# Block-sparse attention and a GELU layer on one core: the last output row in two column pieces, the x of eight pairs transposed by DMA, idle staging tiles reused

## The chip, the cores and the metric

One core of a Trainium2 chip. The metric is the device time of one execution in microseconds, the median of the runs; lower is better. Engines are named as in the profile: PE (TensorE; PEld is its weight load), DVE (VectorE), ACT (ScalarE), POOL (GpSimd) and SP (SyncE, which issues nearly all transfers).

## The reference, cut to what matters

Inputs q, k and v are 4 batches × 8 heads × 768 tokens × 64, in 32 bits. Each query looks at its own block of 64 keys and at the three best of the earlier blocks (by the dot product with the block's mean key), causally. The result is put into rows of 512 (8 heads × 64) and goes through a two-layer network with a hidden width of 2048.

```python
k_rep = k.reshape(B, H, n_blocks, block, D).mean(axis=3)
gate_scores = np.einsum('bhsd,bhnd->bhsn', q, k_rep)
...
top_idx = np.argsort(gate_scores, axis=-1)[..., -top_k:]
...
scores = scale * np.matmul(q, k.transpose(0, 1, 3, 2))
mask = mask & (pos[:, None] >= pos[None, :])
scores = np.where(mask, scores, -1000000000.0)
...
return np.matmul(attn, v).astype(np.float32)
...
h = x @ w_in
c = np.float32(np.sqrt(2.0 / np.pi))
g = 0.5 * h * (1.0 + np.tanh(c * (h + 0.044715 * h * h * h)))
return (g @ w_out).astype(np.float32)
```

## The kernel before, in words

The work is cut into **steps**, and the order in which they are issued is written out by hand in the string `ORDER` (lines 26 to 129). `do` (L979) runs the entries one by one. `u.6.2.0@0` is the step `u.6.2.0` with PSUM slot 0, `xc.8.0:v` the step `xc.8.0` on engine v (a = ACT, v = DVE, p = POOL). Since each engine takes its instructions in order, `ORDER` also sets the order on every engine and on SP's queue of transfers. Tiles come from pools with a fixed number of buffers; a step that needs a buffer waits until its last reader is done.

**Attention.** Two heads make a pair; batch b has the pairs 4b to 4b+3, 16 in all. The first four are worked on in groups of two (names with `0`, L187 to L703). For pairs 4 to 15 the steps are, in the names of `ORDER`:
- `d.p.x` (`load`, L397): q, k and v (x = 0, 1, 2) of the pair, two transfers each, into an `io` tile (pool of 9).
- `hn`, `ln` (L706, L713): q and k as a high and a low 16-bit half, scaled; on POOL, DVE or ACT.
- `zqh`, `zkh`, `zql` (`dma_t`, L723): transposes of these halves by DMA, one instruction on SP's queue for 128 × 768 elements (L728).
- `c0`, `c1` (L733): copies of the transposed q and k into `qk`; `v` (L747): v in 16 bits.
- `s`, `b`, `g`, `m`, `mt`, `mc` (L738 to L817): block sums of k, gate scores, choice of three blocks, transposed mask, mask rows copied into `qk`. `kp`, `gt`, `mt` and `xt` all live in one PSUM bank (pool `small`, one buffer).
- `k`, `x`, `a` (L823 to L862): scores on PE, exponentials on ACT, causal part on POOL. Scores, `pv` and `hps` share three PSUM slots of two banks (`@0` to `@2`).
- `p` (L864): attn times v. `n` (`normalise`, L646): DVE divides and writes `xn` (16 bits, two buffers).
- `xt` (`x_t`, L663): six PE transposes of 128 × 128 into the `small` bank. `xc` (`x_c`, L877): ACT or DVE copies them into `xT`, which holds x transposed, 128 × 4 × 3072.

**The network.** Tokens go in 12 chunks of 256, three to a batch; so chunks 3 to 5 read the pairs 4 to 7, chunks 6 to 8 the pairs 8 to 11, chunks 9 to 11 the pairs 12 to 15.
- `u.ch.dj.half` (`up`, L913): 8 matmuls of 256 columns from `w_in` and `xT` into `hps`; the fourth of each group of four reads the fourth pair of the batch.
- `y.ch.dj` (`gelu`, L930): ACT.
- `f.ch.ti.dj` (`down`, L938): 4 matmuls of 512 columns into `ops`, for row block ti (128 tokens). `ops` comes from the pool `opsp`, one bank.
- `o.ch.ti` (`out_c`, L950): ACT or DVE copies the bank into `osb` (pool of 2). `w.ch.ti` (`out_d`, L955): 256 KB to memory from SP's queue.

The weights come in 32 bits through tiles of the pool `w32` (7 buffers), early in the run. `dmN` (`idle`, L970) is filler for PE in the first 27 us: N matmuls of 128 columns on zeros, 144 in all. The end of `ORDER`:

```
f.11.0.1 f.11.0.2 y.11.3 f.11.0.3 o.11.0:a w.11.0 f.11.1.0 w.10.0 f.11.1.1 f.11.1.2 f.11.1.3
o.11.1:a w.11.1
```

Of the kernel before, what the change touches and what calls it, by code (L numbers as in the profile page):

```python
# [8 lines left out]
FP32 = mybir.dt.float32  # L9
# [32 lines left out]
g.0.2 b.1.2 u.0.2.1 y.0.0 u.0.1.0@1 m.0.2 u.0.1.1 k.1.1.0.0@0 y.0.2 v.0.1.1:p d.4.1 lw.out.3
v.1.1.0:a c.par.0 y.0.1 k.1.1.1.0@2 mt.0.2 cw.in.7:p a.0.1.1 a.1.1.1 hn0.4.0:p ma.1.1.0 p.0.1.0@1
p.0.1.2 cw.out.1:p mc.0.2:v ln0.4.0:v p.0.1.3 p.0.1.1 g.1.2 d0.0.4.2 x.1.1.1.0 x.1.1.0.0 f.0.0.0
n.0.1 k.0.2.1.0@1 k.0.2.0.0@2 ma.0.2.0 d.5.0 a.1.1.0 d0.1.4.2 x.0.2.0.0 v.1.1.1:p p.1.1.0@0 m.1.2
p.1.1.2 p.1.1.1 p.1.1.3 xt.0.1 k.0.2.0.1@2 n.1.1 x.0.2.1.0 hn1.4.0:p cw.out.2:p cw.in.6:p
cw.out.3:v xc.0.1:a k.0.2.1.1@1 ma.0.2.1 zql.4.0 mt.1.2 x.0.2.0.1 v.0.2.0:v mc.1.2:v k.0.2.1.2@0
f.0.0.1 xt.1.1 zqh.4.0 u.0.3.0@2 xc.1.1:v x.0.2.1.1 d.5.1 hn0.5.0:p ln1.4.0:v lw.out.6 d0.0.5.2
ln0.5.0:v k.0.2.0.2@1 ma.0.2.2 u.0.3.1 x.0.2.0.2 lw.out.5 x.0.2.1.2 s.4.0 b.4.0 u.1.0.0@1
u.1.1.0@0 c.ke.0.0:p g.4.0 y.0.3 lw.out.7 u.1.0.1 u.1.1.1 zql.5.0 cw.out.4:v m.4.0 zqh.5.0 zkh.4.0  # L50
u.1.2.0@2 u.1.2.1 hn1.5.0:p a.0.2.1 y.1.0 a.0.2.0 k.1.2.0.0@1 ln1.5.0:v d0.1.5.2 y.1.1 v.0.2.1:a
c.ke.0.1:p cw.out.5:v k.1.2.1.0@0 cw.out.6:p ma.1.2.0 y.1.2 x.1.2.1.0 c.par.1 s.5.0 b.5.0
x.1.2.0.0 p.0.2.0@2 p.0.2.1 p.0.2.2 p.0.2.3 f.0.0.2 mt.4.0 k.1.2.1.1@0 n.0.2 k.1.2.0.1@2 ma.1.2.1
# [79 lines left out]
def kernel(  # L133
# [9 lines left out]
    nc = tc.nc  # L143
    B, H, S, D = q.shape
# [880 lines left out]
```

## Time and profile before

| | us |
|---|---|
| median of 3 runs | 281.26 |
| lowest and highest run | 280.41 and 281.69 |
| profiled execution, first to last instruction | 278.3 |
| PE busy in it | 264.5 (95%) |
| ACT, DVE, POOL busy | 192.8, 139.3, 131.4 |
| `ops` matmuls (L944) and `hps` matmuls (L923) | 95.0 and 92.9 |
| DMA transposes (L728) | 36 |
| transfers of the main queue, share of 16 DMA engines | 65.6% |

The profile shows another execution than the three timed ones, and its span leaves out what lies before the first and after the last instruction; the median is 3.0 us above it. Busy times are unions: a matmul's row gives its whole duration, and since matmuls are pipelined, what one costs is the distance between the starts of two. In the chain of waits such distances are what is shown.

### The profile page before, as it was taken

To read this page: it belongs to the slowest core of one execution; us is meant where nothing else is said; L and a number is where in the kernel's file an instruction comes from. 1 tells how busy PE (TensorE), PEld (TensorE's weight loads), DVE (VectorE), ACT (ScalarE), POOL (GpSimd) and SP (SyncE) were. 2 spreads that over 40 slices of the span, in tenths; PEclk is the share of its full clock that TensorE was granted. 3 is DMA by queue.
4 is the path that set the end of the run, shared out by engine and by line. 5 is a ranking of instruction groups with operands and counts; after the bars stand their busy time and mean duration, and the time that the engine had idled before them with its cause. 6 is when DMAs were issued, how large, how long until landed. Compare 5 with 4: busy or idle time off the path is not lost.

```text
span 278.3 us, 7163 instructions
## 1 busy us (share of the span) xinstructions
PE 264.5 (95%) x2910; PEld 188.8 (68%) x2910; DVE 139.3 (50%) x431; ACT 192.8 (69%) x221; POOL 131.4 (47%) x193
## 2 busy tenths in 40 slices
PE   5899697999999999999999999999999999999994
PEld 5677583865787666886766756786676777756651
DVE  2697458786878686867376466553442010000000
ACT  1568487788699979958898876897887753412330
POOL 6447699899725488870825929400352200000000
PEclk9999799999999999999999999999999999999999
DMA  8998999999699887998998984803112101010102
GB/s 177 272 258 266 346 287 225 245 263 183 110 207 220 181 172 145 204 237 110 169 228 194 245 132 101 166 2 59 39 38 77 40 0 40 38 40 0 75 0 113
DMA packets 107872, 41.09 MB, mean 148 GB/s; under 512 B 96576, under 2 KB 100672, under 8 KB 107840
## 3 DMA queue, kind: packets, MB, share of 16 engines
q1 hardware_dynamic: 105728, 40.12, 65.6%
q10 hardware_dynamic: 2112, 0.52, 1.0%
q8 instruction: 22, 0.36, 0.6%
q14 instruction: 10, 0.08, 0.1%
HBM read 27.26 MB, written 6.29 MB: 121 GB/s over the span
## 4 chain that ended last, share of the span: by engine, by line
PE 84%; DVE 4%; ACT 4%; DMA 3%; POOL 3%; issue 1%; ACTq 0%; DVEq 0%; POOLq 0%
PE ops L944 28%; PE hps L923 28%; PE st L829 9%; PE pv L871 6%; DMA w_in<-in_moe_w_in_dram 3%; PE st L576 2%; PE pv L640 2%; PE dm L976 2%; PE xt L667 1%; PE w L442 1%; ACT qk L448 1%; PE mt L807 1%; PE gt L771 1%; PE kp L742 1%; PE st L594 1%
## 5 line engine op out<-in xcount | busy, mean ns | idle before, releaser
L944 PE MATMUL ops<-w_out,gT 128*128 128x512 f16 x384 | 95.0, 379 | 0.7 <-ACT osb L952 0.7
L923 PE MATMUL hps<-xT,w_in 128*128 128x256 f16 x768 | 92.9, 275 | 0.0
L923 PEld LDWEIGHTS <-w_in 128*128 128x128 f16 x768 | 74.6, 99 | 14.9 <-issue 0.2
L845 ACT ACTIVATE at<-st 128x1024 f16<-128x1024 f32 (+1 forms) x72 | 62.9, 918 | 12.7 <-PE st L829 11.1
L933 ACT ACTIVATE gT<-hps 128x1024 f16<-128x1024 f32 x48 | 47.8, 1024 | 27.8 <-PE hps L923 27.4
L859 POOL TENSOR_SCALAR_AFFINE_SELECT at<-at 128x256 f16<-128x256 f16 x72 | 31.2, 449 | 59.8 <-ACT at L845 57.1
L944 PEld LDWEIGHTS <-gT 128*128 128x128 f16 x384 | 35.7, 97 | 33.4 <-issue 1.9
L184 POOL TENSOR_SCALAR hn<-io 128x768 f16<-128x768 f32 x15 | 34.3, 2284 | 8.6 <-DMA io<-in_q_dram 6.4
L829 PE MATMUL st<-qk 76*128 76x128 f16 (+2 forms) x192 | 36.1, 305 | 0.6 <-ACT at L845 0.5
L952 DVE COPY osb<-ops 128x512 f32<-128x512 f32 x11 | 7.6, 690 | 50.5 <-PE ops L944 47.5
L716 DVE SCALAR_TENSOR_TENSOR ln<-io,hn 128x768 f16<-128x768 f32 x24 | 24.1, 1005 | 1.8 <-POOL hn L184 1.5
L613 ACT ACTIVATE at<-st 128x768 f16<-128x768 f32 (+1 forms) x24 | 20.7, 915 | 6.2 <-PE st L594 6.2
L829 PEld LDWEIGHTS <-qk 76*128 76x128 f16 x192 | 16.6, 97 | 11.8 <-issue 1.1
L871 PEld LDWEIGHTS <-at 128*128 128x128 f16 x504 | 17.4, 97 | 1.8
L871 PE MATMUL pv<-v,at 128*128 128x65 f16 x504 | 18.1, 193 | 0.0
L952 ACT COPY osb<-ops 128x512 f32<-128x512 f32 x13 | 7.6, 585 | 12.3 <-PE ops L944 12.0
L976 PE MATMUL dm<-zsrc 128*128 128x128 f16 x144 | 11.5, 233 | 3.2 <-POOL zsrc L230 3.2
L933 ACT ACT_TABLE_LOAD x11 | 14.1, 1283 | 0.2
L651 DVE RECIPROCAL zrec<-pv 128x12 f32<-128x12 f32 x12 | 2.8, 231 | 19.3 <-PE pv L871 19.1
L976 PEld LDWEIGHTS <-zsrc 128*128 128x128 f16 x144 | 9.6, 105 | 3.9 <-POOL zsrc L230 3.1
L448 ACT ACTIVATE qk<-w 128x1024 f16<-128x1024 f32 x6 | 6.2, 1029 | 8.2 <-DVE ks L464 4.3
L735 POOL COPY qk<-khT 64x768 f16<-64x768 f16 x14 | 11.5, 820 | 0.6
(136 smaller groups left out, 320.4 us busy)
## 6 DMA issues: line engine op xcount, KB each, us to landing
out_dram<-osb SPq DMA_DIRECT2D x24, 256.0 KB, 2.3
io<-in_q_dram SPq DMA_DIRECT2D x24, 192.0 KB, 4.3
io<-in_k_dram SPq DMA_DIRECT2D x24, 192.0 KB, 3.9
io<-in_v_dram SPq DMA_DIRECT2D x24, 192.0 KB, 3.8
w_in<-in_moe_w_in_dram SPq DMA_DIRECT2D x8, 512.0 KB, 6.6
w_out<-in_moe_w_out_dram SPq DMA_DIRECT2D x8, 512.0 KB, 6.6
io<-in_v_dram SPq DMA_DIRECT2D x12, 128.0 KB, 5.3
io<-in_q_dram SPq DMA_DIRECT2D x4, 256.0 KB, 4.9
```

What stands on the lines that cost most here:

```text
L184: math_on[eng].tensor_scalar(out=out, in0=in_, scalar1=c, scalar2=None, op0=ALU.mult)
L613: nc.scalar.activation(out=ov, in_=iv, func=AF.Exp, bias=0.0, scale=SCALE / (QS * QS))
L716: math_on[eng].scalar_tensor_tensor(out=g.rearrange("p t c -> p (t c)"), in0=IO[p, x].rearrange("p t h d -> p (t h d)"), scalar=QS, in1=U[ ...
L829: nc.tensor.matmul(st[:, hh, cb:cb + nq * 128], kt[p % 2][hh][0:64 + NBLK, jc * 128:(jc + 1) * 128], qt[p % 2][hh][0:64 + NBLK, qc * 128:( ...
L845: nc.scalar.activation(out=ov, in_=iv, func=AF.Exp, bias=0.0, scale=SCALE / (QS * QS))
L859: nc.gpsimd.affine_select(out=a, in_=a, compare_op=ALU.is_ge, fill=0.0, base=0, pattern=[[0, 2], [1, 128]], channel_multiplier=-1,)
L871: nc.tensor.matmul(U["pv", p][:, o:o + 65], AT[p, hh, jc, qc], v16[p % NSLOT][:, jc, hh, :], start=(jc == 0), stop=(jc == qc),)
L923: nc.tensor.matmul(hps[:, j * TCH:(j + 1) * TCH], w_in16[:, ci, fi * 128:(fi + 1) * 128], xT[:, ci, t0:t0 + TCH], start=(ci == 0), stop=(c ...
L933: nc.scalar.activation(out=g.rearrange("p a w -> p (a w)"), in_=G["h", ch, dj], func=AF.Gelu_apprx_tanh, bias=0.0, scale=1.0,)
L944: nc.tensor.matmul(G["o", ch, ti], G["g", ch, dj][:, j, ti * 128:(ti + 1) * 128], w_out16[:, fi, :], start=(fi == 0), stop=(fi == NF - 1),)
L952: copy_on[eng](out=osb, in_=G["o", ch, ti])
L976: nc.tensor.matmul(U["dm"][:, 0:128], zsrc, zsrc, start=True, stop=True)
```

## The change

- **x of eight pairs by DMA.** For the pairs 4, 5, 8, 9, 10, 12, 13 and 14 the steps `xt` and `xc` are gone. At the place of `xt` stands `zx` (`x_dma`): one DMA transpose on SP's queue from `xn` into `xT`. Pairs 6, 7, 11 and 15 keep `xt` and `xc`.
- **The last row in two pieces.** Row 1 of chunk 11 is computed as columns 0 to 383 (`f.11.1`, copied by ACT) and then as columns 384 to 511 (`f.11.2`, `o.11.2:v`, `w.11.2`, copied by DVE), each with its own transfer. Row 1 of the chunks 9, 10 and 11 takes the `small` bank in place of the `ops` bank.
- **Idle staging tiles.** v of the pairs 8 to 15 is loaded into a weight tile (`w32`) in place of an `io` tile, and the odd rows of chunks 3 and later are staged in a weight tile in place of `osb`.
- **The filler** issues up to 512 columns with one matmul (the same zeros read up to four times): 40 matmuls for 144, with the same number of columns.
- Nothing else moves in `ORDER`.

```diff
+    XDMA = (4, 5, 8, 9, 10, 12, 13, 14)
+    P32 = 8
+    C32 = 3
...
     def load(p, x):
         b, hp = divmod(p, HP)
-        a = io.tile([128, NC, 2, D], FP32, tag="io", name=f"io_{p}_{x}")
+        if x == 2 and p >= P32:
+            a = w32p.tile([128, 2, 512], FP32, tag="w32", name=f"w32_v_{p}")
+            a = a.rearrange("p a x -> p (a x)")[:, 0:NC * 2 * D].rearrange(
+                "p (t h d) -> p t h d", h=2, d=D)
+        else:
+            a = io.tile([128, NC, 2, D], FP32, tag="io", name=f"io_{p}_{x}")
...
+    def x_dma(p):
+
+        b, hp = divmod(p, HP)
+        nc.sync.dma_start_transpose(
+            out=xT[:, hp, b * S:(b + 1) * S].rearrange(
+                "d (t p) -> d t p", p=128),
+            in_=U["xn", p].rearrange("p t h d -> p (t h d)"))
+
...
-        step(f"xt.{un}", x_t, (p,), NC, p)
-        step(f"xc.{un}", x_c, p)
+        if p not in XDMA:
+            step(f"xt.{un}", x_t, (p,), NC, p)
+            step(f"xc.{un}", x_c, p)
+        else:
+            step(f"zx.{un}", x_dma, p)
...
+    LAST = NCH - 1
+    CUT = 384
+
+    def columns(ch, ti):
+
+        if ch < LAST or ti == 0:
+            return ti, 0, DM
+        return (1, 0, CUT) if ti == 1 else (1, CUT, DM)
+
     def down(ch, ti, dj):
+        row, a, b = columns(ch, ti)
         if dj == 0:
-            G["o", ch, ti] = opsp.tile([128, 512], FP32, tag="ops",
-                                       name=f"ops_{ch}_{ti}")
+            if ch >= LAST - 2 and ti == 1:
+                o = small.tile([128, 512], FP32, tag="small",
+                               name=f"pso_{ch}_{ti}")
+            else:
+                o = opsp.tile([128, 512], FP32, tag="ops",
+                              name=f"ops_{ch}_{ti}")
+            G["o", ch, ti] = o
         for j in range(4):
             fi = 4 * dj + j
             nc.tensor.matmul(
-                G["o", ch, ti],
-                G["g", ch, dj][:, j, ti * 128:(ti + 1) * 128],
-                w_out16[:, fi, :], start=(fi == 0), stop=(fi == NF - 1),
+                G["o", ch, ti][:, a:b],
+                G["g", ch, dj][:, j, row * 128:(row + 1) * 128],
+                w_out16[:, fi, a:b], start=(fi == 0), stop=(fi == NF - 1),
             )
 
     def out_c(ch, ti, eng):
-        osb = otp.tile([128, DM], FP32, tag="osb", name=f"osb_{ch}_{ti}")
-        copy_on[eng](out=osb, in_=G["o", ch, ti])
+        row, a, b = columns(ch, ti)
+        if ch >= C32 and ti % 2:
+            osb = w32p.tile([128, 2, 512], FP32, tag="w32",
+                            name=f"w32_o_{ch}_{ti}")[:, 0]
+        else:
+            osb = otp.tile([128, DM], FP32, tag="osb", name=f"osb_{ch}_{ti}")
+        copy_on[eng](out=osb[:, a:b], in_=G["o", ch, ti][:, a:b])
         G["s", ch, ti] = osb
...
-        for _ in range(n):
-            nc.tensor.matmul(U["dm"][:, 0:128], zsrc, zsrc, start=True,
-                             stop=True)
+        while n > 0:
+            m = min(n, 4)
+            nc.tensor.matmul(
+                U["dm"][:, 0:m * 128].rearrange("p (a x) -> p a x", a=m), zsrc,
+                zsrc.unsqueeze(1).to_broadcast([128, m, 128]), start=True,
+                stop=True)
+            n -= m
```

The end of `ORDER` becomes:

```
f.11.0.1 f.11.0.2 y.11.3 f.11.0.3 o.11.0:a w.11.0 f.11.1.0 w.10.0 f.11.1.1 f.11.1.2 f.11.1.3
o.11.1:a w.11.1 f.11.2.0 f.11.2.1 f.11.2.2 f.11.2.3 o.11.2:v w.11.2
```

More of the change, by code (lines that the diff above doesn't have):

```diff
@@ L42 @@
[L42 to L53, printed above, removed]
@@ new lines @@
+cw.in.3:p l.0.2 ma.1.1.1 lw.in.2 d0.1.2.2 d.4.0 x.1.1.0.1 xt.1.0 x.1.1.1.1 lw.out.2 xc.1.0:v
+t2.1.2@1 cw.in.2:p u.0.0.0@0 u.0.0.1 lw.in.6 lw.out.4 b.0.2 s.1.2 u.0.2.0@2 h2.1.2 l.1.2 g.0.2
+b.1.2 u.0.2.1 y.0.0 u.0.1.0@1 m.0.2 u.0.1.1 k.1.1.0.0@0 y.0.2 v.0.1.1:p d.4.1 lw.out.3 v.1.1.0:a
+c.par.0 y.0.1 k.1.1.1.0@2 mt.0.2 cw.in.7:p a.0.1.1 a.1.1.1 hn0.4.0:p ma.1.1.0 p.0.1.0@1 p.0.1.2
+cw.out.1:p mc.0.2:v ln0.4.0:v p.0.1.3 p.0.1.1 g.1.2 d0.0.4.2 x.1.1.1.0 x.1.1.0.0 f.0.0.0 n.0.1
+k.0.2.1.0@1 k.0.2.0.0@2 ma.0.2.0 d.5.0 a.1.1.0 d0.1.4.2 x.0.2.0.0 v.1.1.1:p p.1.1.0@0 m.1.2 p.1.1.2
@@ new lines @@
+p.1.1.1 p.1.1.3 xt.0.1 k.0.2.0.1@2 n.1.1 x.0.2.1.0 hn1.4.0:p cw.out.2:p cw.in.6:p cw.out.3:v
+xc.0.1:a k.0.2.1.1@1 ma.0.2.1 zql.4.0 mt.1.2 x.0.2.0.1 v.0.2.0:v mc.1.2:v k.0.2.1.2@0 f.0.0.1
+xt.1.1 zqh.4.0 u.0.3.0@2 xc.1.1:v x.0.2.1.1 d.5.1 hn0.5.0:p ln1.4.0:v lw.out.6 d0.0.5.2 ln0.5.0:v
+k.0.2.0.2@1 ma.0.2.2 u.0.3.1 x.0.2.0.2 lw.out.5 x.0.2.1.2 s.4.0 b.4.0 u.1.0.0@1 u.1.1.0@0
+c.ke.0.0:p g.4.0 y.0.3 lw.out.7 u.1.0.1 u.1.1.1 zql.5.0 cw.out.4:v m.4.0 zqh.5.0 zkh.4.0 u.1.2.0@2
+u.1.2.1 hn1.5.0:p a.0.2.1 y.1.0 a.0.2.0 k.1.2.0.0@1 ln1.5.0:v d0.1.5.2 y.1.1 v.0.2.1:a c.ke.0.1:p
@@ new lines @@
+cw.out.5:v k.1.2.1.0@0 cw.out.6:p ma.1.2.0 y.1.2 x.1.2.1.0 c.par.1 s.5.0 b.5.0 x.1.2.0.0 p.0.2.0@2
+p.0.2.1 p.0.2.2 p.0.2.3 f.0.0.2 mt.4.0 k.1.2.1.1@0 n.0.2 k.1.2.0.1@2 ma.1.2.1 c.q0.0 cw.out.7:p
+c0.4.0.1:p mc.4.0.1:v d.6.1 zkh.5.0 d.4.2 f.0.0.3 c0.4.0.0:p mc.4.0.0:v k.1.2.0.2@1 g.5.0
+c.ke.1.1:p x.1.2.0.1 c1.4.0.0:p k.1.2.1.2@2 ma.1.2.2 m.5.0 o.0.0:a c1.4.0.1:p v.1.2.0:v d.6.0
+c0.5.0.0:v c.ke.1.0:p x.1.2.1.2 f.0.1.0 x.1.2.0.2 f.0.1.1 v.1.2.1:v x.1.2.1.1 a.1.2.1 k.4.0.3@2
+f.0.1.2 x.4.0.3 c1.5.0.1:v k.4.0.2@1 a.1.2.0 k.4.0.1@0 f.0.1.3 mt.5.0 mc.5.0.0:v mc.5.0.1:v x.4.0.1
@@ new lines @@
+p.1.2.0@2 o.0.1:v p.1.2.1 a.4.0.3 c0.5.0.1:p p.1.2.3 d.7.1 x.4.0.2 c1.5.0.0:p p.1.2.2 k.4.0.0@0
+x.4.0.0 k.4.0.4@1 n.1.2 xt.0.2 d.7.0 xc.0.2:v f.1.0.0 a.4.0.1 v.4.0:p k.4.0.5@2 k.5.0.3@0 hn0.6.0:a
+xt.1.2 xc.1.2:v x.4.0.5 a.4.0.0 zqh.6.0 a.4.0.2 a.4.0.5 ln0.6.0:v zql.6.0 hn1.6.0:v f.1.0.1
+ln1.6.0:v u.2.0.0@2 x.5.0.3 hn1.7.0:v u.1.3.0@0 x.4.0.4 k.5.0.5@1 u.2.0.1 x.5.0.5 c.q0.1 u.1.3.1
+hn0.7.0:p ln1.7.0:v a.4.0.4 s.6.0 u.2.2.0@1 d.5.2 u.2.2.1 y.2.0 v.5.0:p b.6.0 a.5.0.3 y.1.3 a.5.0.5
+g.6.0 k.5.0.2@2 d.8.0 zkh.6.0 zqh.7.0 w.0.0 y.2.2 ln0.7.0:v k.5.0.1@0 f.1.0.2 p.4.0.0@1 m.6.0
@@ new lines @@
+p.4.0.1 x.5.0.2 f.1.0.3 x.5.0.1 zql.7.0 n.4.0 a.5.0.1 k.5.0.4@2 s.7.0 hn0.8.0:v k.5.0.0@0 b.7.0
+u.2.1.0@1 u.2.1.1 c0.6.0.0:a d.8.1 c0.7.0.1:v o.1.0:v mt.6.0 x.5.0.4 c1.6.0.0:a u.2.3.0@2 zkh.7.0
+x.5.0.0 mc.6.0.1:v mc.6.0.0:a c1.6.0.1:v a.5.0.2 ln0.8.0:v a.5.0.0 u.2.3.1 f.1.1.0 c0.6.0.1:v g.7.0
+y.2.1 k.6.0.2@0 f.1.1.1 w.1.0 y.2.3 x.6.0.2 f.1.1.2 k.6.0.3@1 x.6.0.3 k.6.0.0@2 f.1.1.3 x.6.0.0
+a.5.0.4 m.7.0 zx.4.0 hn1.8.0:p c1.7.0.0:p p.5.0.0@0 p.5.0.1 ln1.8.0:v k.6.0.1@1 x.6.0.1 s.8.0
+o.1.1:v k.6.0.4@2 f.2.0.0 d.6.2 zql.8.0 b.8.0 c0.7.0.0:v mt.7.0 zqh.8.0 a.6.0.2 f.2.0.1 k.6.0.5@1
@@ new lines @@
+w.0.1 a.6.0.3 mc.7.0.0:v n.5.0 x.6.0.4 d.7.2 c1.7.0.1:p mc.7.0.1:a zkh.8.0 x.6.0.5 d.9.0 a.6.0.4
+a.6.0.0 d.10.0 k.7.0.1@2 g.8.0 d.9.1 f.2.0.2 k.7.0.4@1 x.7.0.1 c0.8.0.0:p k.7.0.2@0 x.7.0.4 a.6.0.5
+f.2.0.3 m.8.0 k.7.0.0@2 v.6.0:p c1.8.0.1:v a.6.0.1 x.7.0.2 v.7.0:p p.6.0.0@1 zx.5.0 p.6.0.1
+c0.8.0.1:v a.7.0.4 a.7.0.1 c1.8.0.0:v o.2.0:a k.7.0.3@0 f.2.1.0 mt.8.0 x.7.0.0 x.7.0.3 mc.8.0.1:a
+hn0.9.0:p zqh.9.0 w.2.0 mc.8.0.0:a d.10.1 a.7.0.0 a.7.0.2 f.2.1.1 k.7.0.5@2 f.2.1.2 x.7.0.5
+k.8.0.3@0 a.7.0.3 a.7.0.5 ln0.9.0:v n.6.0 k.8.0.4@1 p.7.0.0@2 hn1.9.0:p x.8.0.3 hn0.10.0:v zql.9.0
@@ new lines @@
+f.3.0.1 b.10.0 y.3.3 x.9.0.3 a.8.0.5 x.9.0.4 k.9.0.0@0 f.3.0.2 ln1.11.0:v g.10.0 p.8.0.0@1 f.3.0.3
+v.9.0:v w.1.1 zkh.10.0 m.10.0 x.9.0.0 o.3.0:a k.9.0.2@2 k.9.0.1@0 p.8.0.1 d.13.1 zkh.11.0 d.12.0
+c1.10.0.0:v f.3.1.0 mt.10.0 x.9.0.2 hn0.11.0:p x.9.0.1 mc.10.0.1:a a.9.0.3 w.3.0 a.9.0.2 a.9.0.1
+a.9.0.0 u.5.0.0@2 f.3.1.1 k.9.0.5@0 u.5.0.1 ln0.11.0:v n.8.0 mc.10.0.0:a c1.10.0.1:p x.9.0.5
+u.4.1.0@1 s.11.0 k.10.0.0@0 u.4.1.1 y.5.0 d.12.1 zqh.11.0 f.3.1.2 y.4.1 u.4.3.0@2 f.3.1.3 zql.11.0
+x.10.0.0 hn0.12.0:v ln0.12.0:v a.9.0.5 c0.11.0.1:p a.9.0.4 hn1.12.0:p d.10.2 o.3.1:v b.11.0
@@ new lines @@
+c1.11.0.1:v k.10.0.2@1 u.4.3.1 u.5.1.0@0 y.4.3 d.12.2 d.13.0 zql.12.0 g.11.0 u.5.1.1 c1.11.0.0:a
+f.4.0.0 y.5.1 k.10.0.4@2 f.4.0.1 c0.11.0.0:a x.10.0.2 p.9.0.0@0 ln1.12.0:v m.11.0 p.9.0.1 mt.11.0
+v.10.0:v mc.11.0.1:v mc.11.0.0:v w.2.1 f.4.0.2 f.4.0.3 k.10.0.3@1 s.12.0 n.9.0 x.10.0.4 k.11.0.0@2
+o.4.0:a zkh.12.0 zqh.12.0 d.11.2 k.10.0.5@0 b.12.0 zx.9.0 x.10.0.3 hn0.13.0:p f.4.1.0 a.10.0.2
+x.10.0.5 k.11.0.3@1 k.10.0.1@0 f.4.1.1 zx.8.0 x.11.0.0 x.10.0.1 d.14.2 w.3.1 d.14.1 c0.12.0.0:a
+x.11.0.3 hn1.13.0:p c0.12.0.1:p a.11.0.0 ln1.13.0:v f.4.1.2 u.5.3.0@2 k.11.0.2@0 g.12.0 f.4.1.3
@@ new lines @@
+a.10.0.3 u.5.2.0@1 u.5.2.1 u.5.3.1 a.10.0.0 d.14.0 x.11.0.2 v.11.0:p a.10.0.1 d.15.0 zkh.13.0 w.4.0
+d.15.1 y.5.2 m.12.0 o.4.1:a a.10.0.4 a.10.0.5 p.10.0.0@0 p.10.0.1 mt.12.0 n.10.0 mc.12.0.1:v
+k.11.0.1@1 f.5.0.0 f.5.0.1 c1.12.0.1:p y.5.3 hn1.14.0:p c1.12.0.0:p zqh.13.0 mc.12.0.0:a s.13.0
+x.11.0.1 k.11.0.5@2 k.11.0.4@0 ln1.14.0:v b.13.0 x.11.0.4 a.11.0.2 a.11.0.1 x.11.0.5 f.5.0.2 s.14.0
+k.12.0.3@1 zkh.14.0 k.12.0.5@0 f.5.0.3 a.11.0.5 a.11.0.4 a.11.0.3 hn0.14.0:p ln0.13.0:v x.12.0.3
+b.14.0 k.12.0.0@2 p.11.0.0@1 zx.10.0 w.4.1 x.12.0.5 x.12.0.0 o.5.0:v p.11.0.1 k.12.0.1@0 hn1.15.0:v
@@ L129 @@
+f.10.0.0 u.11.0.1 w.10.1 f.10.0.1 f.10.0.2 y.11.0 w.9.1 u.11.3.0@1 f.10.0.3 u.11.1.0@0 u.11.1.1
+u.11.3.1 o.10.0:v f.11.0.0 y.11.2 y.11.1 f.11.0.1 f.11.0.2 y.11.3 f.11.0.3 o.11.0:a w.11.0 f.11.1.0
+w.10.0 f.11.1.1 f.11.1.2 f.11.1.3 o.11.1:a w.11.1 f.11.2.0 f.11.2.1 f.11.2.2 f.11.2.3 o.11.2:v
+w.11.2
 """
@@ L661, in normalise @@
         U["xn", *key] = xn
+        U["xn", key[0]] = xn
     def x_t(key, nt, un):
@@ L963 @@
             step(f"y.{ch}.{dj}", gelu, ch, dj)
-        for ti in range(TCH // 128):
+        for ti in range(TCH // 128 + (ch == LAST)):
             for dj in range(4):
```

115 lines of the change are left out of this document (34 added, 81 removed).

## The prediction

> **What bounds the kernel now.** I read the page first, then a table of windows, then TensorE's own waits. The page gives the span, TensorE's share, and the DMA engines' busy tenths in 40 slices of 6.96 us:
>
> ```profile
> span 278.3 us, 7163 instructions
> PE 264.5 (95%) x2910; PEld 188.8 (68%) x2910; DVE 139.3 (50%) x431; ACT 192.8 (69%) x221; POOL 131.4 (47%) x193
> DMA  8998999999699887998998984803112101010102
> ```
>
> The windows say where the other 5% lies. Columns: stretch, its length, then busy us of PE, PEld, DVE, ACT, POOL, granted clock, DMA share, GB/s.
>
> ```profile
> 75.00:156.00 81.00, 80.91 (x919) 58.38 (x917) 55.28 (x163) 70.82 (x80) 48.83 (x60) 1.00 0.99 188
> 156.00:175.00 19.00, 18.34 (x227) 12.98 (x226) 11.90 (x33) 14.47 (x17) 12.28 (x18) 1.00 0.82 151
> 175.00:270.50 95.50, 95.49 (x853) 66.70 (x851) 21.49 (x69) 55.23 (x62) 12.74 (x27) 1.00 0.15 42
> 270.50:278.30 7.80, 3.61 (x16) 1.46 (x15) 0.00 (x0) 1.17 (x2) 0.00 (x0) 1.00 0.26 101
> ```
>
> From 75 us to 270.5 us TensorE stands idle for 0.76 us in all. A busy PE need not be at its peak, so I checked the pace in the chain of waits: `ops` comes at 3.47 us for 16 matmuls of 512 columns (quoted below), 217 ns each, and nothing in that stretch is slower. So every column taken from TensorE there shortens the kernel, as long as nothing else is late in its place. The last 7.8 us are a serial tail. The start, up to 45 us, waits on transfers, and the diff touches it only in the filler matmuls.
>
> What TensorE waited for after 75 us:
>
> ```profile
> PE ops L944 <- ACT osb L952: 0.7, 1, 0.7
> PE st L829 <- ACT at L845: 0.5, 2, 0.3
> PE kp L742 <- ACT qk L816: 0.2, 1, 0.2
> ```
>
> The first row is the single output bank: row 11.1 waits until ACT has copied row 11.0.
>
> **The x path: eight pairs leave TensorE.** Removed are 8 × 6 transposes of 128×128 and eight copies to `xT` (three on ACT, five on DVE). Price of the transposes, from the group's row and from the chain, where a group of six stands between neighbours without a gap:
>
> ```profile
> L667 PE MATMUL xt<-ident,xn 128*128 128x128 f16 x72 | 6.0, 219 | 0.0
> 93.93 0.34 PE xt L667 x6
> 94.27 1.28 PE pv L871 x42
> 110.01 0.34 PE xt L667 x6
> ```
>
> One transpose lasts 219 ns from start to end, but six take 0.34 us of TensorE's time (93.93 + 0.34 is where the next begins), 57 ns each. Eight groups are 8 × 0.34 = **2.7 us**. All eight lie between 93 us and 222 us, where TensorE is full. I take the whole of it; the bounds are 0 (all re-spent in waits) and 2.7.
>
> The Trainium skill, "TensorE: Matmul & The Clock Gate", Part 4 (PE-mode transpose), gives about 275 ns for a 128×128 transpose inside a kernel; by it 48 would be worth 13.2 us. The trace's pitch of 57 ns speaks against it; even the single duration is 219 ns.
>
> The copies are worth nothing by themselves: in these stretches ACT and DVE are busy less than TensorE and mostly wait for it (ACT 70.8 of 81 us, DVE 55.3). What goes is eight holds of the one `small` bank, for which no row above shows TensorE waiting.
>
> **What is added in their place** is eight DMA transposes on SP's queue. The trace has 36 like them. First their time to landing, then two alone on the queue, as a window:
>
> ```profile
> DMA to landing us min/median/max: 2.7/3.5/6.9
> 186.90:193.00 6.10, 6.10 (x78) 4.28 (x76) 2.18 (x5) 4.14 (x6) 0.00 (x0) 1.00 0.34 65
> ```
>
> 6.10 × 0.34 / 2 = 1.04 us of all DMA engines each. Their issue keeps SP for 1.2 to 1.4 us (rows below). Each also waits in SP's queue for its `normalise` on DVE, with loads and other transposes behind it. Deadlines, first where the queue and the engines have room:
>
> ```profile
> 98.92 1.63 SPq L401 DMA_DIRECT2D io<-in_k_dram  x2
> 105.47 1.21 SPq L728 DMA_TRANSPOSE qhT<-hn  x1
> 112.97 0.88 PE hps L923 x8
> 214.03 0.96 DVE L655 TENSOR_TENSOR xn<-pv,zrec 128x768 f16<-128x768 f32 x1
> 228.65 1.91 PE L923 MATMUL hps<-xT,w_in 128*128 128x256 f16 x16
> ```
>
> - Pairs 4 and 5: pair 4 goes out near 87 us, pair 5 in SP's pause from 100.6 to 105.5, which also takes up the delay of pair 4; chunk 4 first reads them at 112.97. No cost.
> - Pairs 12 to 14: the DMA engines are nearly idle (0.15 from 175 us on). Pair 14 is the last: `xn` ends at 215.0, plus at most 6.9 makes 222, and chunk 9 starts at 228.65. No cost.
> - Pairs 8, 9 and 10 go out between 148 and 164 us, where the DMA engines are full (the slices from 146 to 167 us show 8, 9, 8). This is the only place with a price:
>
> ```profile
> 146.29 3.86 SPq L401 DMA_DIRECT2D io<-in_v_dram  x4
> 149.04 0.96 DVE L655 TENSOR_TENSOR xn<-pv,zrec 128x768 f16<-128x768 f32 x1
> 151.06 1.12 SPq L401 DMA_DIRECT2D io<-in_k_dram  x2
> 157.83 2.13 POOL L184 TENSOR_SCALAR hn<-io 128x768 f16<-128x768 f32 x1
> 159.91 0.82 POOL L735 COPY qk<-khT 64x768 f16<-64x768 f16 x1
> 160.96 1.41 SPq L728 DMA_TRANSPOSE khT<-hn  x1
> 163.07 0.69 ACT qk L816
> 165.84 1.21 SPq L728 DMA_TRANSPOSE qlT<-ln  x1
> 173.61 1.75 PE hps L923 x16
> 175.36 0.25 PE gt L771 x10
> ```
>
> `zx.9` and `zx.8` come in the middle of the four value loads. `xn` of pair 9 ends at 150.0, so SP stands up to 1.8 us; SP's transfers take eight semaphores in turn, so up to eight are still outstanding, and what is lost is their own work, 2 × 1.04 = 2.1 us, and 3.1 us after `zx.10`. Who is behind: the key load of pair 14 (151.06, landing about 4 us later at 155) is read by POOL's `hn1.14` at 157.83: 2.8 us of slack. Behind that on POOL is the key copy of pair 12, done at 160.7, which the scores need only with the mask rows that ACT finishes at 163.76: 3 us more. The `qlT` of pair 13 (165.84, landing at 169 to 170) is needed by the gate at 175.36: 5 us. `zx.10` issues near 164, lands at 167.5 to 171, and is read from 173.6. A lag of 2 to 3 us fits into each, also with TensorE arriving 1.3 to 1.7 us earlier. I take **0**; the bounds are 0 and 2 us (the 6.9 us landing in place of 3.5 for `zx.10`, less the slack).
>
> **The idle staging tiles.** The value loads of pairs 8 to 15 and the odd output rows go into weight tiles. They take the same instructions; fewer tiles compete for `io` and `osb`. Loads follow SP's order and the DMA rate, not the tiles, so I take 0 and no loss.
>
> **The filler.** 144 matmuls of 128 columns become 40 of up to 512. The pace before and the place in the chain:
>
> ```profile
> 12.60 1.07 PE L976 MATMUL dm<-zsrc 128*128 128x128 f16 x16
> 26.74 8.33 DMA w_in<-in_moe_w_in_dram
> ```
>
> (1.07 − 0.22) / 15 = 57 ns for 128 columns, against 217 / 4 = 54 ns by wide ones: 0.4 us for all 144 if each were on the path, and the path leaves TensorE at 26.7 us for a transfer of 8.3 us. I take 0; bounds −0.4 and 0.
>
> **The tail.** Now, from the chain and the timeline:
>
> ```profile
> 267.04 3.47 PE ops L944 x16
> 270.53 0.59 ACT osb L952
> 271.17 3.63 PE ops L944 x16
> 274.86 0.59 ACT osb L952
> DMA to landing us min/median/max: 2.0/2.3/4.4
> L555 ACT COPY mrow<-mt 128x128 f16<-128x128 f16 x2 | 0.5, 268 | 0.7 <-PE mt L546 0.7
> L784 DVE TENSOR_TENSOR ga<-gt,cgate 128x120 f32<-128x120 f32 x12 | 3.4, 282 | 10.2 <-PE gt L771 10.1
> ```
>
> Count from X = 270.5, the end of row 11.0. Before: bank wait 0.67, matmuls to X+4.3, copy X+4.36 to X+4.95, transfer and close 2.85, end X+7.8. After: row 11.1 has the `small` bank and starts at X. Its 384 columns cost 16 × 0.163 = 2.6 us, the last 128 columns 16 × 0.057 = 0.9 us (the transposes' pitch, since they too load weights each time): X+3.5, drained at X+3.7. ACT copies the first piece beside that (X+2.9 to X+3.4; about 0.5 us between its 0.27 for 128 columns and 0.59 for 512) and SP issues it by X+3.8. DVE copies 128 columns in about 0.28 us, done at X+4.0. Its transfer is a quarter of the bytes; I take 2.65 for the 2.85. End X+6.7: **1.1 us** less. Bounds: 0.7 (the bank wait alone) and 1.5.
>
> The Trainium skill, "DMA: Bandwidth & Descriptors", Rules for kernel authors, says that transfers under 64 KB pay mostly overhead; by it the last piece, 64 KB, lands hardly sooner than 256 KB did, and the tail would gain 0.9 us rather than 1.1. The 2.0 us minimum for 256 KB above neither shows nor excludes that.
>
> **Sum.** 2.7 + 1.1 = 3.8 us: span 278.3 to 274.5. The runs' median is 281.26, 3.0 us above this span (the frame around it and other executions); with the same frame, 281.26 − 3.8 = **277.5 us**.
>
> **The rivals.**
> - *Part of the DMA lag comes back.* Between 155 and 175 us one of the four slacks is 1 to 2 us too short and TensorE waits that long. For it: the engines are full there, and POOL, ACT and DVE run in order, so one late load holds what is behind. Against: the slacks above. 278.5 to 279.8.
> - *Slower: the queue stops around a transpose.* If on a full queue each of the three (8, 9, 10) held everything behind for its whole landing, median 3.5, instead of 1.04, the lag would be 10.5 us; less 4 us of slack TensorE waits 6.5 us: 284. It decides against the change from a lag of about 9 us (4 slack, 3.8 gain, 1.4 threshold). Against it: after `khT` at 160.96 SP goes on at 162.4, and the two transposes of the window at 187 us run 1.4 us apart.
> - *TensorE gets ahead and waits.* ACT has 70.8 of 81 us before 156; if ACT and POOL set the pace as soon as TensorE is 2.7 us ahead, only the tail is left: 280.2. Against: their idle time is waiting for TensorE, so they move with it.
> - *A transpose is worth its duration.* 48 × 0.219 = 10.5 us and the tail: 269.7. Against: the chain's 0.34 us for six. The skill's 275 ns points this way.
>
> **Chances.** Sum as worked out 0.63; lag comes back 0.22; slower 0.07; only the tail 0.06; duration 0.02. The range 276.3 to 279.9 takes in the first two with the bounds of the tail and a few tenths of scatter, about 0.84. Half a per cent (1.4 us) is about what a measurement can tell from no change: faster by more than that 0.86, within it 0.07, slower 0.07.
>
> **What would show it.** Right: `xt` has 24 matmuls of pairs, not 72; TensorE is full from 75 us to the end of row 11.2; no wait of `ops` for ACT; last copy about 0.28 us on DVE; span near 274.5. Wrong: TensorE waiting at `kp`, `gt`, `st` or `hps` between 150 and 175 us, with POOL's `hn` or a `qlT` released by a DMA just before; chunk 3, 6 or 9 waiting for a transfer into `xT`; or a tail of more than 7 us after row 11.0.

## The result and the profile after

| | before | after |
|---|---|---|
| median of the runs made together, us | 281.39 (4 runs) | 277.63 (4 runs: 277.60, 277.62, 277.64, 280.04) |
| ratio of the times | | 0.9884, 95% interval 0.9841 to 0.9927 |
| span of the profiled execution | 278.3 | 275.0 |
| `xt` transposes of the later pairs on TensorE, DMA transposes | 72, 36 | 24, 44 |
| from the end of row 11.0 to the end | 7.8 | 6.4 |

Faster by 1.2%, 277.6 us where 277.5 was forecast. (The ratios here and below are the recorded estimates with their intervals, not quotients of the medians beside them.) The changed kernel was run twice more beside other kernels (ratios 0.9886, interval 0.984 to 0.9932, and 0.9875, interval 0.9838 to 0.9911); its 16 runs reach from 276.06 to 280.04 us, median 278.4. Where this scatter sits is an experiment below.

The page of the changed kernel: the span, the busy engines and the DMA engines' tenths.

```profile
span 275.0 us, 6896 instructions
PE 261.8 (95%) x2774; PEld 181.4 (66%) x2774; DVE 135.8 (49%) x427; ACT 190.6 (69%) x218; POOL 131.3 (48%) x193
DMA  7999999999799997999996999912205211100203
```

TensorE is busy 2.7 us less and its share is still 95%: what it lost in work, the kernel lost in length. The windows of the changed kernel (stretch, length, busy us of PE, PEld, DVE, ACT, POOL, granted clock, DMA share, GB/s):

```profile
75.00:156.00 81.00, 80.83 (x912) 57.90 (x910) 51.92 (x161) 71.70 (x81) 48.96 (x61) 1.00 1.05 188
156.00:175.00 19.00, 18.34 (x225) 13.04 (x224) 11.88 (x33) 14.44 (x17) 13.51 (x19) 1.00 1.11 204
175.00:270.50 95.50, 95.50 (x832) 66.13 (x830) 21.12 (x69) 53.44 (x60) 12.00 (x25) 1.00 0.21 52
```

Three of the DMA transposes go out where the queue is full:

```profile
150.18 2.54 SPq L887 DMA_TRANSPOSE xT<-xn  x2
166.67 1.21 SPq L887 DMA_TRANSPOSE xT<-xn  x1
```

Between 156 and 175 us, behind the first two and around the third, the DMA share rose from 0.82 to 1.11, and TensorE is busy 18.34 us of 19 in both kernels. Nothing was re-spent there. TensorE's own waits in the changed kernel from 75 us to 270 us:

```profile
PE st L836 <- ACT at L852: 0.5, 2, 0.3
PE kp L749 <- ACT qk L823: 0.2, 1, 0.2
```

These two were there before; the wait of `ops` for ACT is gone, and no wait for a transfer into `xT` came. The end of the chain of waits in the changed kernel (start, us, what):

```profile
265.16 3.45 PE ops L977 x16
268.61 2.60 PE pso L977 x16
271.21 0.91 PE ops L977 x16
272.19 0.29 DVE osb L990
```

`pso` is row 11.1's first piece in the `small` bank: it starts where row 11.0 ends, 268.61. The two pieces take 2.60 and 0.91, and the last copy is the 0.29 us of DVE.

**Where the 3.3 us of span come from.** I matched the matmuls of two traces one by one and compared their starts, so that each shift says how far TensorE's work lies ahead or behind:

| the same place | before | after | shift |
|---|---|---|---|
| first scores of the later pairs | 65.95 | 66.52 | +0.57 |
| end of row 11.0 | 270.51 | 268.61 | −1.90 |
| end of the span | 278.3 | 275.0 | −3.3 |

From 66 us to the end of row 11.0 that is 2.47 us gained, in the tail 1.4, and ahead of 66 us 0.6 lost. The experiments test these three.

### The profile page after: what moved, and what is told of

Its sections match the earlier page's. It is cut to its first block, busy times and chain, and to the rows that moved or that the text cites. A ratio compares the mean times of both kernels' runs of the same rounds, so it can differ in the third digit from the quotient of the medians.

```text
span 275.0 us, 6896 instructions
## 1 busy us (share of the span) xinstructions
PE 261.8 (95%) x2774; PEld 181.4 (66%) x2774; DVE 135.8 (49%) x427; ACT 190.6 (69%) x218; POOL 131.3 (48%) x193
## 4 chain that ended last, share of the span: by engine, by line
PE 74%; DMA 9%; ACT 5%; DVE 4%; POOL 3%; SPq 3%; issue 1%; DVEq 0%; POOLq 0%; ACTq 0%
PE hps L941 27%; PE ops L977 23%; PE st L836 8%; PE pv L878 5%; DMA w_in<-in_moe_w_in_dram 5%; PE pso L977 3%; DMA io<-in_k_dram 3%; DMA io<-in_q_dram 1%; SPq L407 1%; PE mt L814 1%; ACT qk L454 1%; ACT at L852 1%; PE kp L749 1%; PE pv L646 1%; PE gt L778 1%
## 5 line engine op out<-in xcount | busy, mean ns | idle before, releaser
L977 PE MATMUL ops<-w_out,gT 128*128 128x512 f16 (+1 forms) x352 | 85.0, 371 | 0.5 <-POOL w_out L338 0.5
L977 PEld LDWEIGHTS <-gT 128*128 128x128 f16 x400 | 36.8, 97 | 32.8 <-issue 1.5
L866 POOL TENSOR_SCALAR_AFFINE_SELECT at<-at 128x256 f16<-128x256 f16 x72 | 32.0, 461 | 54.1 <-ACT at L852 53.6
L185 POOL TENSOR_SCALAR hn<-io 128x768 f16<-128x768 f32 x15 | 33.5, 2232 | 9.9 <-DMA io<-in_k_dram 5.5
L723 DVE SCALAR_TENSOR_TENSOR ln<-io,hn 128x768 f16<-128x768 f32 x24 | 24.9, 1036 | 3.0 <-POOL hn L185 2.8
L990 DVE COPY osb<-ops 128x512 f32<-128x512 f32 (+1 forms) x7 | 4.4, 632 | 42.7 <-PE ops L977 42.6
L1016 PE MATMUL dm<-zsrc 128*128 128x512 f16 (+3 forms) x40 | 11.3, 390 | 3.1 <-POOL zsrc L231 3.1
L661 DVE TENSOR_TENSOR xn<-pv,zrec 128x768 f16<-128x768 f32 x12 | 11.5, 957 | 0.4
L823 DVE COPY qk<-mt 12x640 f16<-12x640 f16 x15 | 7.3, 486 | 8.3 <-PE mt L814 8.1
```

What stands on the lines that cost most here:

```text
L185: math_on[eng].tensor_scalar(out=out, in0=in_, scalar1=c, scalar2=None, op0=ALU.mult)
L661: nc.vector.tensor_tensor(out=xn[:, 0:nt].rearrange("p c h d -> p h c d"), in0=pz[:, :, :, 0:64], in1=zrec[:, :, 0:nt].unsqueeze(3).to_bro ...
L723: math_on[eng].scalar_tensor_tensor(out=g.rearrange("p t c -> p (t c)"), in0=IO[p, x].rearrange("p t h d -> p (t h d)"), scalar=QS, in1=U[ ...
L866: nc.gpsimd.affine_select(out=a, in_=a, compare_op=ALU.is_ge, fill=0.0, base=0, pattern=[[0, 2], [1, 128]], channel_multiplier=-1,)
L977: nc.tensor.matmul(G["o", ch, ti][:, a:b], G["g", ch, dj][:, j, row * 128:(row + 1) * 128], w_out16[:, fi, a:b], start=(fi == 0), stop=(fi ...
```

## The experiments

Ratios are to the kernel before on the same chip (median 281.7, 281.4 and 281.7 us in the three rounds of experiments).

| kernel | median us | ratio, 95% interval |
|---|---|---|
| x alone | 278.97 | 0.9907 (0.988 to 0.9934) |
| tail alone | 280.20 | 0.9942 (0.9914 to 0.9971) |
| bank alone | 281.46 | 0.9985 (0.9958 to 1.0011) |
| staging and filler alone | 281.91 | 1.0013 (0.9995 to 1.0032) |
| x and tail | 277.49 | 0.9852 (0.9819 to 0.9885) |
| all twelve pairs by DMA | 286.38 | 1.0168 (1.0133 to 1.0203) |
| three transposes each | 285.43 | 1.0149 (1.0105 to 1.0193) |
| the changed kernel again | 279.27 | 0.9886 (0.984 to 0.9932) |
| more filler | 278.22 | 0.9881 (0.9856 to 0.9905) |
| the changed kernel, third time | 278.36 | 0.9875 (0.9838 to 0.9911) |

### x alone

The kernel before with this edit only:

```diff
+XDMA = (4, 5, 8, 9, 10, 12, 13, 14)
-xt.4.0 ... xc.4.0:v
+zx.4.0
...
```

> Only the x of the eight pairs goes by DMA; tail, banks, staging tiles and filler are as before. Theory (a group of six transposes costs TensorE 0.34 us, the DMA lag costs nothing): 8 x 0.34 = 2.7 us less, 278.7 us beside 281.4; TensorE's work comes early by 0.34 us more behind each missing group, and the tail after row 11.0 keeps its 7.8 us. Rival (lag comes back): 0.7 to 1.7 us less, with a wait of TensorE between 150 and 175 us. Rival (TensorE gets ahead and waits for ACT or POOL): within 0.5 us of before. Rival (a transpose is worth its 219 ns): 10.5 us less.

Measured: 278.97 us, 2.7 us less than 281.71. The matched matmuls lie 1.31 us behind those of before at 66 us and 1.14 us ahead at the end of row 11.0: 2.45 us. The shift comes in steps: 0.10 at pair 4, then seven times 0.33 to 0.34. The waits and the end of the chain are those of before:

```profile
PE ops L976 <- ACT osb L989: 0.7, 1, 0.7
```

```profile
265.90 3.47 PE ops L976 x16
269.37 0.02 issue
269.39 0.59 ACT osb L989
269.98 0.04 issue
270.02 3.63 PE ops L976 x16
```

The theory holds, and the rivals by which the DMA lag comes back or TensorE only waits longer fall: with the pace set by ACT there would have been no steps of 0.33. A transpose is not worth its 219 ns either.

**Why the first group gave 0.10 and not 0.34.** The timeline of the changed kernel there:

```profile
93.51 2.85 ACT L852 ACTIVATE at<-st 128x1024 f16<-128x1024 f32 x3
94.58 1.10 PE L878 MATMUL pv<-v,at 128*128 128x65 f16 x31
```

The first of the three exponentials, `x.6.0.2`, lasts 1.02 us by itself (the next starts a little before it ends) and ends at 93.51 + 1.02 = 94.53. By `ORDER` it reads PSUM slot 0 (`k.6.0.2@0`), which `p.5.0.0@0` takes next: `pv` starts at 94.58. Before, the transposes of pair 4 filled most of this wait. A removed piece of work is worth only what it takes beyond the wait that it covers.

### Tail alone and bank alone

Tail alone is the kernel before with both edits below, bank alone with the first:

```diff
+            if ch >= LAST - 2 and ti == 1:
+                o = small.tile([128, 512], FP32, tag="small",
...
+        return (1, 0, CUT) if ti == 1 else (1, CUT, DM)
```

> Only the last row is split at column 384, and row 1 of chunks 9 to 11 takes the small bank; all else as before. Theory: from the end of row 11.0 to the end 6.4 to 6.7 us in place of 7.8, so 1.1 to 1.4 us less, about 280.1 beside 281.4. Rival (the bank alone counts, the piece lands no sooner): 0.7 us less. Rival (what the tail gives depends on the x path): under 0.3 us less.

> Only the bank: row 1 of chunks 9 to 11 takes the small bank, the last row stays whole with 512 columns, all else as before. Theory: the wait of 0.67 us between row 11.0 and row 11.1 goes and nothing else, tail 7.1 us in place of 7.8, about 280.7 beside 281.4. Rival (the split gives all of the tail's gain): tail 7.8 us, no change.

Measured: 280.20 and 281.46 us. The second is 0.25 us less than before where 0.7 was expected, and within its interval of no change. The recorded spans, which leave out the time outside the first and last instruction, tell it apart: median 278.85 us of its 12 runs against 279.8 us of the 27 runs of before, 0.95 less (95% interval of the difference of the means, by resampling, 0.4 to 1.4). What hid it in the times lies outside the span: a median of 2.5 us in its runs and of 1.7 in those of before. The size of it is in the profile. The window of the tail alone from the end of row 11.0, then the chain's end of the bank alone:

```profile
270.82:277.20 6.38, 3.49 (x32) 2.35 (x30) 0.29 (x1) 1.06 (x2) 0.00 (x0) 1.00 0.34 123
```

```profile
269.05 3.45 PE ops L977 x16
272.50 3.47 PE pso L977 x16
...
276.04 0.58 ACT osb L990
```

The tail alone ends 6.38 us after row 11.0, as in the changed kernel. With the bank alone, row 11.1 starts at once (269.05 + 3.45 = 272.50), and the span of 279.5 ends 7.0 us after. So of 1.4 us the bank gives 0.8 and the split 0.6. From the end of the last copy to the end of the span it is 279.5 − 276.62 = 2.88 us for 256 KB and 275.0 − 272.48 = 2.52 for 64 KB in the changed kernel.

The Trainium skill, "DMA: Bandwidth & Descriptors", Rules for kernel authors, has transfers under 64 KB pay mostly overhead. The last piece has 64 KB, just at that bound. The 2.52 of 2.88 us that a quarter of the bytes still takes agrees with it, though the other 0.36 us counted here.

### Staging and filler alone; x and tail

The first is the kernel before with `P32 = 8`, `C32 = 3` and the wide filler; the second is the changed kernel without them:

```diff
-    P32 = 8
-    C32 = 3
+    P32 = 99
+    C32 = 99
...
-            m = min(n, 4)
+            m = 1
```

> Only the staging tiles and the wide filler; x path, tail and banks as before. Theory: nothing, 281.4 within 0.5 us. Rival: the trace of the changed kernel has TensorE's work 0.2 us earlier up to 34 us and 0.4 to 0.6 us later at 47 to 66 us than before; if the filler or the tiles cause that, this kernel shows the same two steps and is about 0.6 us longer. If they don't, the steps are scatter of the transfers from one execution to the next, and here they come out otherwise.

> The changed kernel without the idle staging tiles and with the filler of before: the x path and the tail alone. Theory (tiles and filler are worth nothing): as the changed kernel, 277.6 within 0.5 us. Rival (tiles and filler cost the 0.2 to 0.6 us that the changed kernel's trace shows late at 47 to 66 us): 277.2 or less and below the changed kernel in the same job.

Measured: 281.91 us (interval −0.05% to +0.32%) and 277.49 us. Worth nothing as forecast; a cost of some tenths cannot be excluded (the median span is 0.4 us longer than that of before, with an interval of −0.1 to 0.8 for the means). The median of x and tail is the lowest of all, but its interval overlaps those of the changed kernel, so it isn't shown to be better. At 66 us, both lie 1.37 us behind before, one with the wide filler, one without: the late start is not the filler's.

### All twelve pairs by DMA

```diff
-    XDMA = (4, 5, 8, 9, 10, 12, 13, 14)
+    XDMA = (4, 5, 6, 7, 8, 9, 10, 11, 12, 13, 14, 15)
```

> The changed kernel, but the pairs 6, 7, 11 and 15 go by DMA too; nothing else. In the changed kernel xn of pair 7 is done at 111.4 us and chunk 4 reads it from about 113.3, and pair 11 stands as near to chunk 7. Theory (a transfer pays only where the first reader is some 4 us away): four more groups save 4 x 0.33 = 1.3 us, but a DMA transpose issued at 111.5 lands 2.7 to 3.5 us later at the soonest, so TensorE waits about 1.5 to 3 us ahead of chunk 4 and as long ahead of chunk 7, less at pair 15: 2 to 5 us longer than the changed kernel, 280 to 283 us. Rival (the landing is hidden here too): 1.3 us shorter than the changed kernel, 276.5 us.

Measured: 286.38 us, some 8 us longer than the changed kernel, more than expected. Of this kernel TensorE's waits from 75 us to 270 us, a piece of the chain, and three windows:

```profile
PE hps L941 <- DMA xT<-xn: 5.9, 4, 3.7
```

```profile
113.59 4.08 DMA xT<-xn
117.67 0.04 issue
117.71 1.23 PE hps L941 x5
```

```profile
113.00:117.71 4.71, 0.68 (x6) 0.31 (x4) 1.45 (x1) 3.07 (x3) 2.31 (x2) 0.87 0.95 99
117.71:123.30 5.59, 5.59 (x37) 4.06 (x37) 1.92 (x4) 1.02 (x1) 3.71 (x6) 0.50 1.07 212
123.30:128.00 4.70, 4.70 (x53) 4.23 (x51) 2.37 (x15) 2.52 (x3) 2.82 (x6) 0.99 1.24 245
```

The transpose of pair 7 is issued at 113.59, lands 4.08 us later, and chunk 4, ready at 117.71 − 3.66 = 114.05, waits 3.7 us for it. Part of this is the queue: pair 7's `xn` was done at 112.10, but the transpose of pair 6 (110.90) and a `qhT` (112.26) stood ahead on SP. What I had left out comes behind: after that wait the granted clock is 0.50 for 5.6 us. Against the changed kernel, the matmuls fall back by 0.5 us in a first short wait for pair 6, by 3.8 us in this wait and by 2.6 us more in the half-speed stretch; pairs 11 and 15 add waits of 0.9 and 1.3 us. That the landing is hidden here too falls.

The Trainium skill, "TensorE: Matmul & The Clock Gate", Part 1, says that TensorE runs at half rate after an idle window of about 3.4 us and needs about 3.4 us of work to come back. The trace agrees in kind; behind the wait the half rate lasted 5.6 us here. The length of the idle time does not agree: in the tail alone, a wait of 1.9 us near 29 us, with little work behind it, was followed by a granted clock of 0.50 too.

### Three transposes each for the pairs 8, 9 and 10

```diff
+        if p in (8, 9, 10):
+            t = io.tile([128, 2, NC, 128], FP16, tag="io", name=f"spare_{p}")
+            for e in range(2):
+                nc.sync.dma_start_transpose(
+                    out=t[:, e],
+                    in_=U["xn", p].rearrange("p t h d -> p (t h d)"))
```

> The changed kernel, but behind each of the DMA transposes of the pairs 8, 9 and 10 two more of the same data go into spare tiles that nobody reads: between 148 and 167 us nine transposes where the changed kernel has three and the kernel before none. Theory (each costs the queue and the DMA engines 1.04 to 1.4 us, and there are 2.8 to 5 us of slack): a lag of 9 x 1.04 = 9.4 us at pair 13 in place of 3.1, or up to 12 by issue time, of which 4 to 5 are slack: TensorE waits 3 to 8 us between 155 and 178 us, 280.5 to 286 us. Rival (the lag does not reach TensorE, for its slack is larger than worked out): 277.6. Rival (a transpose holds the queue for its landing of 3.5 us): 18 us more lag, over 290 us.

Measured: 285.43 us. This asks how near the changed kernel stands to the point where the lag comes back. First SP and POOL in the changed kernel, in the timeline:

```profile
154.88 1.10 SPq L407 DMA_DIRECT2D io<-in_k_dram  x2
159.69 2.13 POOL L185 TENSOR_SCALAR hn<-io 128x768 f16<-128x768 f32 x1 [2.17 <-DMA io<-in_k_dram]
```

Then the same load and `hn` with three transposes each, and TensorE's wait and two windows of that kernel:

```profile
162.57 2.87 SPq L407 DMA_DIRECT2D io<-in_k_dram  x2
168.78 2.13 POOL L185 TENSOR_SCALAR hn<-io 128x768 f16<-128x768 f32 x1 [8.92 <-DMA io<-in_k_dram]
```

```profile
PE kp L749 <- POOL at L866: 5.3, 1, 5.3
```

```profile
164.00:172.78 8.78, 3.32 (x28) 1.58 (x27) 2.52 (x5) 4.18 (x5) 4.00 (x4) 0.78 0.98 224
172.78:180.00 7.22, 7.22 (x73) 4.92 (x73) 5.24 (x10) 2.63 (x4) 6.92 (x9) 0.56 0.98 168
```

This execution was 2.3 us behind the changed kernel already ahead of 150 us. So the load goes out 162.57 − 154.88 − 2.3 = 5.4 us later, for four more transposes ahead of it: 1.3 us each, the issue time; `hn` starts 168.78 − 159.69 − 2.3 = 6.8 us later; and `kp` on TensorE 5.5 us later. The profile names POOL's `at`, but the load is what came late: the late `hn` releases `ln` on DVE (170.94 to 172.49), and behind `ln` stands the read of the `small` bank (until 172.71) that `kp` at 172.76 has to wait for. 6.8 − 5.5 = 1.3 us of slack were left. Then TensorE loses another 2 us at a granted clock of 0.56. So the lag rival describes what happens, and in the changed kernel's trace it stood 1.3 us away. That a transpose holds the queue for its landing falls.

### More filler, and the changed kernel again

The changed kernel was run beside others twice, once next to a version with filler in TensorE's first long wait:

```diff
         for x in range(2):
+            if (g, c, x) == (1, 2, 1):
+                idle(40)
             for j in range(2):
```

> The changed kernel itself, beside the others on one chip: 277.6 us within 0.8. Its start up to 66 us is expected to differ by some tenths from its first trace (scatter of the transfers), while from 66 us to the end of row 11.0 the removed groups give 2.4 to 2.5 us again and the tail after row 11.0 is 6.4 us.

> The changed kernel with 40 more filler columns-of-128 (ten matmuls of 512 columns on zeros, 2.2 us) in the middle of the last step of transposed weights, where TensorE waits 2.1 to 3.4 us for POOL near 29 us and then runs at a granted clock of 0.5 until 34 to 38 us. Theory (the start scatters because a long wait is followed by half clock, and where the wait is longest TensorE itself is then the path to 44 us): the clock stays near 1.0 from 28 to 38 us, the slowest executions lose 1 to 2 us and the median comes to 276.3 to 277.5, below the changed kernel in the same job. Rival (the start is set by the transfers and POOL alone, TensorE has room): same as the changed kernel, 277.6 to 279.3. Rival (the filler comes in the way of the work behind it): up to 1 us longer.

> The changed kernel once more, to stand beside the kernel with the longer filler on the same chip: 277.6 to 279.3 us; behind 66 us its profile is expected to agree with its other two within 0.1 us (2.4 to 2.5 us less than before up to row 11.0, tail 6.4), and all its scatter to lie ahead of 66 us.

Measured: 279.27, 278.22 and 278.36 us. The first lies above the 277.6 ± 0.8 that was expected: of its six runs, two had spans of 277.7 and 277.9 us, and two spent 2.8 and 3.0 us outside the span. Two windows of the changed kernel's first trace, then the same of the version with more filler and a third one of it:

```profile
30.00:32.00 2.00, 1.08 (x5) 1.00 (x6) 0.00 (x0) 0.00 (x0) 2.00 (x5) 0.66 1.00 338
32.00:34.00 2.00, 2.00 (x12) 1.40 (x10) 0.83 (x2) 1.18 (x2) 1.06 (x2) 0.50 1.07 351
```

```profile
30.00:32.00 2.00, 1.91 (x13) 1.06 (x11) 0.10 (x1) 0.00 (x0) 1.95 (x4) 1.00 1.05 379
32.00:34.00 2.00, 2.00 (x21) 1.78 (x20) 0.91 (x2) 1.36 (x2) 1.06 (x2) 1.00 1.12 349
43.80:47.20 3.40, 3.27 (x47) 2.32 (x48) 1.39 (x12) 1.59 (x2) 1.31 (x2) 0.50 0.96 222
```

The filler does keep the clock at 1.00 here, and the median is the same as the changed kernel's beside it (278.22 and 278.36). TensorE's work is 1.5 us ahead of before at 35 us and 1.8 us behind at 50 us. A half clock comes later instead (43.80 to 47.20), but behind it TensorE still waits for the casts of `w_out` on POOL (1.6 us in two waits), so it did not set the pace there either. My theory that the half clock near 31 us sets the start falls; a half clock in the start was moved by this filler and not removed. The chain of the version with more filler shows what sets it in that execution:

```profile
26.20 7.80 DMA w_in<-in_moe_w_in_dram
34.05 1.05 POOL w_in L338
...
36.76 9.07 DMA io<-in_k_dram
45.98 2.13 POOL hn L185
48.11 1.53 POOL w_out L338
```

Transfers and POOL: a key load that lands after 9.07 us. The changed kernel's first trace has the same piece with 7.87 us, before's chain has none there. What makes such a load late in one execution and not in another stays open.

**In the traces, all scatter lies ahead of 66 us.** Of each profiled execution: the shift against before at 66 us, the gain from there to the end of row 11.0, and the time from there to the end of the span.

| kernel | shift at 66 us | gain from 66 us to row 11.0's end | tail |
|---|---|---|---|
| before | 0 | 0 | 7.8 |
| changed, three traces | +0.57, −0.11, +1.91 | 2.47, 2.48, 2.48 | 6.4, 6.4, 6.4 |
| more filler | +1.97 | 2.47 | 6.4 |
| x and tail | +1.37 | 2.48 | 6.4 |
| x alone | +1.31 | 2.45 | 7.8 |
| tail alone | +0.31 | 0.00 | 6.4 |
| bank alone | +2.01 | 0.02 | 7.0 |
| staging and filler alone | +1.37 | 0.00 | 7.7 |

What lies behind 66 us repeats to a few hundredths, whatever stands in the start. The times of the runs scatter by more than their spans: what lies outside the span took 1.67 to 3.13 us in the executions on record. The median span of the changed kernel's 16 runs is 276.1 us and that of the 49 runs of before in the rounds of experiments is 279.7 (278.6 to 281.4): 3.6 us, where the traces have 3.9 behind 66 us. The missing 0.3 is not told from scatter of the start.

## Why the prediction was right

- **TensorE bounds it.** Right: each group that left moved all that comes after it, by 0.33 to 0.34 us in seven of eight places, in the traces of the changed kernel and of x alone.
- **x path, 2.7 us.** Measured 2.47. The step's one mis-sized place is "I take the whole of it", with "nothing in that stretch is slower" behind it: the group of pair 4 stood ahead of a wait of 0.25 us for an exponential.
- **Eight DMA transposes, 0 of 0 to 2.** Right by measurement, and the chain was the one described: key load of pair 14 late on SP by 3.8 us (151.06 to 154.88), `hn` on POOL by 1.9 (157.83 to 159.69), TensorE not. The slack left was 1.3 us: not the several us that "a lag of 2 to 3 us fits into each" suggests. The price is 1.3 us of SP per transpose, not 1.04 of the DMA engines, and SP stood for `xn` of pair 9 from 147.22 to 150.18, 3.0 us and not "up to 1.8". The 0 was right by a smaller margin than was worked out.
- **Staging and filler, 0.** Not told from nothing.
- **Tail, 1.1 us.** Measured 1.4. The copy ended at X+3.9 where X+4.0 was forecast, and its transfer closed in 2.52 us where I took 2.65. The Trainium skill's rule on small transfers gave 0.9.
- **Sum, 3.8 us.** 2.47 + 1.4 = 3.9 behind 66 us in every trace. The runs gave 3.8, 2.1 and 3.4 us of difference of medians in the three comparisons, and the medians of the spans differ by 2.95 and 3.2 us in the last two: the start scatters by some 2 us from one execution to the next, and the time outside the span by up to 1.4. The forecast of the span took its gain from the trace with the shortest span of before on record (278.3, the 49 others 278.6 and more), and came to 274.5 where 275.0 was traced and 276.1 is the median. The forecast of the time took it from a median of three runs, 3.0 us above that span. That 277.5 met 277.63 to a tenth is partly luck, the gain behind 66 us isn't.
- **Rivals.** "Lag comes back" and "only the tail" fell with the steps in x alone; "a transpose is worth its duration" fell with 0.33 us per six; "the queue stops around a transpose" fell with 1.3 us of lag per transpose.

## What to carry to other kernels

Work taken from the engine that bounds a stage is worth its pitch in the chain, 57 ns per transpose here and not its 219 ns, less the wait that it covered. A transfer that takes over such work must land before its reader: with 6 us from issue to reader (pair 10) it cost nothing; with 0.5 us (pair 7 in the kernel with all twelve) TensorE lost 3.8 us in the wait and 2.6 more at half clock behind it. Where runs scatter, compare their spans beside their times (so the bank's 0.95 us came out), match the instructions of two traces and look at where the shift changes: gains of 0.3 us could be read to hundredths while the medians moved by 2 us.

## What the runs showed of the hardware

- A wait of 3.7 us on TensorE was followed by 5.6 us at a granted clock of 0.50: 2.6 us more. After a wait of 1.9 to 3.4 us near 29 us the same happens in all traces but the one with filler in it, where it comes at 43.80 us.
- These stretches of half clock had few lengths: 3.4 us around waits of 1.9 to 2.6 us, 6.8 us around waits of 3.0 to 3.7 us (the start of x alone, bank alone, x and tail; pair 7 above, 116.50 to 123.30), and 10.2 us around the wait of 5.3 us (168.90 to 179.10). They began 1.4 to 3.3 us after the wait's start, at times behind its end. The wait alone does not decide: the stretch at 43.80 followed one of 1.1 us, and waits of 1.1 us at that place in other traces were followed by none.
- The time outside the span was 1.7 to 1.8 us in eight of the eleven profiled executions behind the prediction and 2.6 to 2.9 in three, the changed kernel's first among them (277.6 − 275.0).
